# k^T v on both partition halves: by products through the identity, or by copies

## The chip, the cores and the metric

The kernel runs on one core of a Trainium2 chip. A core has a matrix engine (TensorE, PE in the profile; PEld is its loading of weights), VectorE (DVE), ScalarE (ACT), GpSimd (POOL) and SyncE (SP), which here only issues transfers. Each engine works through its own instructions in order and waits on semaphores that the others raise. TensorE writes only to PSUM, a small memory of banks; ScalarE and VectorE read it from there. The metric is the time of one execution on the device in microseconds (us); lower is better.

## The reference

Attention without a softmax over 8 batches of 8 heads, 576 positions and 64 channels, then a mixture of eight experts on its output:

```python
kv = np.einsum('bhsd,bhse->bhde', k, v)
out = np.einsum('bhsd,bhde->bhse', q, kv)
rms = np.sqrt(np.mean(out * out, axis=-1, keepdims=True) + 1e-06)
x = (out / rms * g_norm)           # then (B,H,S,D) -> (B*S, H*D)
...
skip_score = x @ w_skip; logits = x @ w_gate
...
out[do_compute] = x + gate_w * (relu(x @ w1[e]) @ w2[e])
```

All of the change is in the first line and in what the second reads: the 64 x 64 matrix kv of each head. Everything is in fp32.

## The kernel before

The kernel has an attention stage (up to about 118 us) and an expert stage. Its order of instructions is written out by hand: inside `tc.manual_schedule()` each engine gets its instructions in the order of the program text, and the framework adds the semaphores.

**kv of a batch.** `state(b, some)` forms k^T v of the eight heads of batch b on TensorE, in 72 products of 64 x 64 (line 380) into the PSUM tile `sum_ps`. There is one such tile. A product in fp32 shows as two records in the profile. When the last is done, two ScalarE copies (line 387) put the sums into `own(b, w)`: heads with w = 0 into partitions 0 to 63 of the tile `kvd`, heads with w = 1 into partitions 64 to 127. `kvd` holds for each head a block diagonal matrix of two blocks, one per partition half, so that one product of 128 rows can serve two positions at once; so the same numbers have to stand on the other half as well (`kvds[b % KVD][o, :, w, 1 - w, :]`). Beside kv each block has 2 x 9 more columns ("ends"), kv times the weights of the skip score and of the eight gates, so that the routing comes out of the same product as the attention.

Three functions finish a batch:
- `state_t(b)`: four products with the identity (line 394) turn kv into `kvT_ps`, a ScalarE copy takes it to `kvT` (line 397).
- `state_m(b)`: two products of kvT with the gate weights (line 403) give the ends in `lg_ps`, two small ScalarE copies (line 406) put them into `own`.
- `state_s(b)`: two products with the identity (line 412) move the finished block, 292 columns with its ends, to the other partition half in PSUM (`sw_ps`), and two ScalarE copies (line 416) put it into `kvd`.

**Units.** The second line of the reference runs in 36 units n, four per batch and two extra ones after every four batches (units 16, 17, 34, 35) for the ninth block of positions. A unit has these parts: `turn(n)`, four transposes of q (line 461) and a ScalarE copy to qT (line 464); `values(n)`, four products of 128 rows (line 499; line 509 for the extra units) into a bank of `o_ps`, of which there are two, and a ScalarE square of them (line 515); in a batch's first two units two more transposes (line 480) and a copy (line 483) prepare the ninth block. Then `squares(n)` (VectorE reduction, line 523), `root(n)` (ScalarE, line 530), `norm(n)` (VectorE reciprocal and scaling into `xl`, lines 537 and 546, which frees the bank), and `finish(n)` on GpSimd (lines 598 to 616). The stores follow.

**The loop's order.** Step n of the main loop issues: turn(n+1), root(n-1), the jobs put at "early", values(n), the jobs at "mid", norm(n-1) and squares(n), the jobs at "pe", finish(n-1), the jobs at "dve" and "end". The kv work of the batches is spread over the steps as such jobs: the table `portions` says at which step the products of a batch begin and how many go in each step. state_t stands in the step behind the last of them: step 3, 7, 10, 14, 20, 24, 28 for b = 1 to 7. A batch's values begin at n = 4, 8, 12, 18, 22, 26, 30. The next batch's products begin at step 4, 7, 11, 16, 20, 24, so for b = 2, 5 and 6 they start in the step of that batch's own state_t. The gating of tokens (line 663 and on) runs beside this as further jobs, mostly on VectorE with small products on TensorE.

**Loads.** SyncE issues all loads of k, v and q in quarters of a batch (line 118), with three buffers for k and v and two for q, the stores, and later the experts' weights.

Of the kernel before, what the change touches and what calls it, by code (L numbers as in the profile page):

```python
# [17 lines left out]
def kernel(  # L18
# [43 lines left out]
    nc = tc.nc  # L62
    B, H, S, D = q.shape
# [10 lines left out]
    G = E + 1  # L74
# [4 lines left out]
    PK = 2 * KD  # L79

    KVD = 5
# [28 lines left out]
    g_ps = ps_g.tile([P, 512], FP32)  # L110
# [17 lines left out]
    def load_kv(b, js=range(4)):  # L128
        if b < B:
            if js.start == 0:  # L130
                for name, to in (("k", kts), ("v", vts)):
                    to[b] = kv_pool.tile([P, 4, C, D], FP32, tag=name, name=name)
            for j in js:
                for src, t in ((k, kts[b]), (v, vts[b])):
                    load_part(t, src, b, j)

    def load_q(b):
        if b < B:
            qts[b] = load(q_pool, "q", q, b)
# [61 lines left out]
    ident = keep.tile([P, P], FP32)  # L201
# [3 lines left out]
    kvds = []  # L205
# [27 lines left out]
    for a in range(2):  # L233
        r = slice(a * 64, (a + 1) * 64)
# [60 lines left out]
    for lo, m, _ in runs:  # L295
# [26 lines left out]
        out=srow[:, :].rearrange("p (r c) -> p r c", c=CK),  # L322
# [33 lines left out]
    def own(b, w):  # L356

        return kvds[b % KVD][w * 64:(w + 1) * 64, :, w, w, :]

    sum_all = ps_kv.tile([P, 2, 512], FP32, name="sum_ps")  # L360
    sum_ps = sum_all[:, :, 0:2 * D].rearrange("p a (u d) -> p a u d", u=2)
    sw_ps = g_ps[:, 0:2 * PK]
    kvT_ps = g_ps[:, 0:2 * P].rearrange("p (u x) -> p u x", u=2)
    lg_ps = g_ps[:, 2 * PK:2 * PK + 8 * G].rearrange("p (u a w g) -> p u a w g", u=2, a=2, w=2)

    def ends_of(x):

        ap = [list(d) for d in x.ap]
        assert ap[-1] == [1, PK]
        return bass.AP(x.tensor, x.offset, ap[:-1] + [[PK - G, 2], [1, G]])  # L370

    def state(b, some):

        kt, vt = kts[b], vts[b]
        for i in some:
            u, c = divmod(i, C)
            for w in range(2):
                for a in range(2):
                    r = slice(a * 64, (a + 1) * 64)
                    nc.tensor.matmul(  # L380
                        out=sum_ps[w * 64:(w + 1) * 64, a, u, :],
                        lhsT=kt[r, 2 * u + w, c, :], rhs=vt[r, 2 * u + w, c, :],
                        start=(c == 0), stop=(c == C - 1), skip_group_check=True)
        if some.stop < 2 * C:
            return
        for w in range(2):
            nc.scalar.copy(out=own(b, w)[:, :, G:G + 2 * D].rearrange("p u (a d) -> p a u d", a=2),
                           in_=sum_ps[w * 64:(w + 1) * 64, :, :, :])

    def state_t(b):  # L390
        for u in range(2):
            for w in range(2):
                r = slice(w * 64, (w + 1) * 64)
                nc.tensor.matmul(out=kvT_ps[:, u, r], lhsT=kvds[b % KVD][:, u, w, w, G:G + 2 * D],  # L394
                                 rhs=ident[:, r], start=True, stop=True)
        kvT = att_pool.tile([P, 2, P], FP32, tag="kvT", name="kvT", bufs=1)
        nc.scalar.copy(out=kvT[:, :, :], in_=kvT_ps)
        kvTs[b] = kvT

    def state_m(b):  # L400
        kvT = kvTs.pop(b)
        for u in range(2):
            nc.tensor.matmul(out=lg_ps[:, u, :, :, :], lhsT=kvT[:, u, :], rhs=gw_b[:, u, :, :, :],
                             start=True, stop=True)
        for w in range(2):
            nc.scalar.copy(out=ends_of(own(b, w)), in_=lg_ps[w * 64:(w + 1) * 64, :, :, w, :])

    def state_s(b):

        for w in range(2):  # L410
            r, o = slice(w * 64, (w + 1) * 64), slice((1 - w) * 64, (2 - w) * 64)
            nc.tensor.matmul(out=sw_ps[o, :], lhsT=ident[r, r], rhs=own(b, w), start=True, stop=True,  # L412
                             skip_group_check=True)
        for w in range(2):
            o = slice((1 - w) * 64, (2 - w) * 64)
            nc.scalar.copy(out=kvds[b % KVD][o, :, w, 1 - w, :],
                           in_=sw_ps[o, :].rearrange("p (u k) -> p u k", u=2))


    units = []  # L420
# [22 lines left out]
    def at(step, part, job):  # L443
        todo.setdefault((step, part), []).append(job)
# [7 lines left out]
    def turn(n):  # L452
        _, b, i, u = units[n]
        if i is None:
            qTs[n] = q8s[b][:, u, :, :, :]
            return
        ps = ps_q.tile([P, 2, 2, 2, 64], FP32, tag="q", name="q_ps")
        for w in range(2):
            for hf in range(2):
                c = 4 * i + 2 * hf  # L460
                nc.tensor.transpose(out=ps[:, w, :, hf, :], in_=qts[b][:, 2 * u + w, c:c + 2, :],  # L461
                                    identity=ident[:, :])
        qT = att_pool.tile([P, 2, 2, P], FP32, tag="qT", name="qT")
        nc.scalar.copy(out=qT[:, :, :, :].rearrange("p w a t -> p (w a t)"),
                       in_=ps[:, :, :, :, :].rearrange("p w a h t -> p (w a h t)"))
        qTs[n] = qT
# [478 lines left out]
    for b in range(KNOWN // S // 4 * 4, KNOWN // S):  # L945
        nc.gpsimd.dma_start(
            out=out[b * S:(b + 1) * S, :].rearrange("(p c) d -> p c d", c=C)[:, C - 1, :],
            in_=zero)

    starts = {}  # L950
    for n, (_, b, i, _) in enumerate(units):
        if i is not None:
            starts.setdefault(b, n)
    state(0, range(C))
    dense(4)
    state(0, range(C, 2 * C))
    dense(5)
    state_t(0)
    turn(0)
    state_m(0)  # L960
    turn(1)
    state_s(0)

    portions = {1: (1, (10, 8)), 2: (4, (6, 6, 6)), 3: (7, (5, 6, 7)), 4: (11, (5, 6, 7)),
                5: (16, (8, 4, 3, 3)), 6: (20, (4, 4, 5, 5)), 7: (24, (4, 4, 5, 5))}
    over = 0
    for b, n in starts.items():
        if b:
            step, counts = portions[b]
            i = 0  # L970
            for count in counts:
                at(step, "early" if step in (starts[1], starts[2], starts[4] - 2) else "pe",
                   lambda b=b, some=range(i, i + count): state(b, some))
                i += count
                step += 1
            assert i == 2 * C and step < n and step - len(counts) > over - 1
            last = b == B - 1
            at(step, "mid" if last else "early", lambda b=b: state_t(b))
            at(*((step + 1, "early") if last else (step, "pe")), lambda b=b: state_m(b))
            at(step + 1, "early" if step + 1 == n else "pe", lambda b=b: state_s(b))  # L980
            over = step
        at(over, "end", lambda b=b: load_kv(b + 3, range(4 if b else 2)))

        at(n + 2, "end", lambda b=b: load_q(b + 2))
        if b == 0:
            at(n + 2, "end", lambda: load_kv(3, range(2, 4)))
# [73 lines left out]
    with tc.tile_pool(name="wpool_b", bufs=1, reuse_waits="tile") as wpool_b, \  # L1060
# [522 lines left out]
        with tc.If(n_rounds > 1):  # L1583
            with tc.For_i(1, n_rounds, 1):
# [8 lines left out]
                    out=left[:, :].rearrange("p (r c) -> p r c", c=CK),  # L1593
# [39 lines left out]
```

## Time and profile before

| | |
|---|---|
| three runs | 370.62, 371.28 (median), 371.82 us |
| the profiled execution | 372.36 us, of which the span from the first to the last instruction is 370.6 us |
| granted TensorE clock | 0.999 of full speed |
| TensorE busy | 358.2 us, 97% of the span |
| VectorE, ScalarE, GpSimd busy | 242.3, 151.5, 118.6 us (65%, 41%, 32%) |
| from 20 to 60 us: TensorE busy per 10 us | 9.63, 10.00, 10.00, 9.93 |
| the same, ScalarE | 6.21, 6.76, 7.29, 7.14 |
| the same, VectorE | 5.28, 5.64, 4.99, 6.52 |
| from 90 to 120 us: VectorE per 10 us | 8.76, 8.00, 8.91 |
| the same, ScalarE | 7.79, 6.92, 7.75 |
| line 412 (state_s), TensorE | 32 records, 0.405 to 0.457 us each |
| line 416, ScalarE copies of 292 columns | 16, 0.397 to 0.400 us each |
| line 387, ScalarE copies of 256 columns | 16, 0.371 to 0.378 us each |

A busy share is an average over the whole span and over stages with different limits; it does not say what sets the end. The chain that ended last does: from the last instruction it goes back, at each step, to what released it or to the instruction before it on its engine. In rows of the chain the first number is the start in us from the span's beginning and the second how long the piece lasts; "issue" is time in which the engine waited for nothing that the profile shows. In rows of a timeline the brackets give how long the engine was idle before and which instruction ended that. Records of matmuls overlap, since they are pipelined and their ends are modelled; the distance from one start to the next is the better measure of what a group costs.

### The profile page before, as it was taken

The page shows a single profiled execution, that of the slowest core. Times are in us where ns is not written, and L with a number is a line of the kernel's source. Part 1 is how long each engine was busy: PE and PEld are TensorE (multiplying, and loading weights), DVE is VectorE, ACT ScalarE, POOL GpSimd, SP SyncE. Part 2 cuts the span into 40 slices and gives each one's busy share as a digit, 9 for nine tenths or more (in the row PEclk, how much of TensorE's full clock was granted, in tenths as well). Part 3 has the DMA queues.
Part 4 walks back from the last instruction along what each step waited for, and adds up shares of the span by engine and source line. Part 5 has one row for each costly group of instructions (what it writes and reads, how often), then busy time and mean ns, then how long its engine had stood idle before and what let it go on. Part 6 is the DMA issues. An engine that isn't in the chain of part 4 may idle for free.

```text
span 370.6 us, 9688 instructions
## 1 busy us (share of the span) xinstructions
PE 358.2 (97%) x3835; PEld 312.8 (84%) x3835; DVE 242.3 (65%) x621; ACT 151.5 (41%) x426; POOL 118.6 (32%) x189
## 2 busy tenths in 40 slices
PE   8999999899999998999999999999999999999994
PEld 4688998798889667589879988988988988999983
DVE  3255557767878761786847675776776876878831
ACT  2467676666767151434303511431530430441420
POOL 8036466655777062223021203303203202002003
PEclk9999999999999999999999999999999999999999
DMA  8999999999598449963617355563662672701001
GB/s 267 387 389 389 396 391 381 385 369 351 182 307 315 113 139 375 384 216 120 227 44 261 79 214 170 189 229 99 222 251 70 232 251 71 240 2 43 17 1 54
DMA packets 32809, 81.72 MB, mean 221 GB/s; under 512 B 3242, under 2 KB 3250, under 8 KB 32756
## 3 DMA queue, kind: packets, MB, share of 16 engines
q1 hardware_dynamic: 28944, 69.48, 53.0%
q0 software_dynamic: 3792, 11.53, 9.4%
q8 instruction: 32, 0.52, 0.6%
q14 instruction: 21, 0.17, 0.1%
q10 hardware_dynamic: 20, 0.02, 0.0%
HBM read 66.80 MB, written 14.48 MB: 219 GB/s over the span
## 4 chain that ended last, share of the span: by engine, by line
PE 83%; issue 6%; DMA 5%; ACT 2%; POOL 2%; DVE 1%; SPq 1%; POOLq 0%; ACTq 0%; DVEq 0%
PE bank L1257 45%; PE bank L1189 9%; PE o_ps L499 7%; PE sum_ps L380 4%; PE bank L1177 4%; PE q_ps L461 3%; PE bank L1158 2%; DMA v<-in_v_dram 2%; PE g_ps L394 2%; DMA q<-in_q_dram 2%; DMA k<-in_k_dram 1%; PE o_ps L480 1%; PE g_ps L857 1%; PE g_ps L412 1%; PE q_ps L857 1%
## 5 line engine op out<-in xcount | busy, mean ns | idle before, releaser
L1267 ACT COPY p<-bank 128x128 f32<-128x128 f32 (+6 forms) x70 | 20.9, 298 | 96.2 <-PE bank L1257 94.7
L1257 PE MATMUL bank<-xt,w 128*128 128x128 f32 (+5 forms) x336 | 55.5, 288 | 0.5 <-DVE bank L1261 0.5
L1388 POOL DMA_INDIRECT out_dram<-xg,rows x14 | 14.0, 1000 | 116.6 <-DVE xg L1385 114.4
L616 POOL TENSOR_TENSOR xb<-xl,g_b 128x512 f32<-128x512 f32 x34 | 41.3, 1216 | 29.6 <-DVE rs L537 27.7
L1257 PEld LDWEIGHTS bank<-xt,w 128*128 128x128 f32 x336 | 47.0, 190 | 2.4 <-DVE bank L1261 1.9
L1261 DVE TENSOR_TENSOR bank<-bank,p 128x128 f32<-128x128 f32 (+6 forms) x70 | 23.6, 337 | 30.0 <-PE bank L1257 28.9
L499 PE MATMUL o_ps<-kvd,qT 128*128 128x146 f32 x240 | 36.0, 290 | 1.1 <-issue 0.8
L1257 PE MATMUL bank<-xs,s 128*128 128x128 f32 (+5 forms) x224 | 36.7, 288 | 0.0
L523 DVE TENSOR_REDUCE rs<-sq 128x8 f32<-128x512 f32 x36 | 24.5, 681 | 15.7 <-ACT sq L515 15.6
L499 PEld LDWEIGHTS o_ps<-kvd,qT 128*128 128x128 f32 x240 | 31.6, 189 | 1.7 <-issue 1.1
L1257 PEld LDWEIGHTS bank<-xs,s 128*128 128x128 f32 x224 | 31.1, 190 | 1.0 <-issue 0.5
L1189 PE MATMUL bank<-w,ht 128*32 128x128 f32 (+2 forms) x424 | 29.9, 313 | 0.0
L546 DVE TENSOR_TENSOR xl<-o_ps,rs 128x584 f32<-128x584 f32 x32 | 24.5, 767 | 4.3 <-DVE rs L537 0.5
L1189 PEld LDWEIGHTS bank<-w,ht 128*32 128x32 f32 (+2 forms) x424 | 18.2, 119 | 10.6 <-issue 7.2
L1257 PE MATMUL bank<-t,ht 128*128 128x256 f32 x112 | 27.0, 384 | 0.0
L1257 PE MATMUL bank<-w,ht 128*128 128x256 f32 x112 | 26.5, 380 | 0.0
L515 ACT ACTIVATE sq<-o_ps 128x512 f32<-128x512 f32 x34 | 20.3, 597 | 15.1 <-PE o_ps L499 14.9
L380 PE MATMUL sum_ps<-v,k 64*64 64x64 f32 x1152 | 25.3, 222 | 0.8 <-DMA v<-in_v_dram 0.8
L1257 PE MATMUL bank<-t,hs 128*128 128x256 f32 x112 | 25.3, 379 | 0.0
L380 PEld LDWEIGHTS sum_ps<-v,k 64*64 64x64 f32 x1152 | 21.6, 134 | 4.3 <-issue 2.2
L1149 POOL DMA_INDIRECT xg<-out_dram,src x14 | 14.0, 998 | 34.9 <-DMA out_dram<-xg,rows 12.7
L1257 PEld LDWEIGHTS bank<-t,ht 128*128 128x128 f32 x112 | 20.8, 190 | 3.9 <-issue 1.2
(217 smaller groups left out, 676.5 us busy)
## 6 DMA issues: line engine op xcount, KB each, us to landing
w<-in_moe_w_dram SPq DMA_DIRECT2D x16, 2048.0 KB, 14.1
k<-in_k_dram SPq DMA_DIRECT2D x32, 288.0 KB, 6.0
v<-in_v_dram SPq DMA_DIRECT2D x32, 288.0 KB, 7.2
q<-in_q_dram SPq DMA_DIRECT2D x32, 288.0 KB, 5.7
out_dram<-xb SPq DMA_DIRECT2D x29, 256.0 KB, 6.0
out_dram<-xb POOLq DMA_DIRECT2D x7, 256.0 KB
xg<-out_dram,src POOLq DMA_INDIRECT x16, 3.4
out_dram<-xg,rows POOLq DMA_INDIRECT x16, 2.5
```

The source lines that it names most:

```text
L380: nc.tensor.matmul(out=sum_ps[w * 64:(w + 1) * 64, a, u, :], lhsT=kt[r, 2 * u + w, c, :], rhs=vt[r, 2 * u + w, c, :], start=(c == 0), stop ...
L499: mm = nc.tensor.matmul(out=ps[:, w, 0:2 * PK].rearrange("p (r k) -> p r k", r=2)[:, :, cols], lhsT=qT[:, w, a, :], rhs=kvds[b % KVD][:, u ...
L515: nc.scalar.activation(out=sq[:, :, :, :], in_=heads(ps, G, G + 2 * D), func=ACT.Square)
L523: nc.vector.tensor_reduce(out=rs[:, :, :], in_=sq[:, :, :, :].rearrange("p x y (a d) -> p x (y a) d", a=2), axis=AX.X, op=ALU.add)
L546: nc.vector.tensor_tensor(out=xl[:, :, :, :].rearrange("p x y (a k) -> p x (y a) k", a=2), in0=ps[:, :, 0:2 * PK].rearrange("p x (h k) -> ...
L616: late.append((lambda eng: eng.tensor_tensor(out=xb[:, :, 4 * u * D:(4 * u + 4) * D].rearrange("p r (w x) -> p r w x", w=2), in0=xl[:, :, ...
L1149: nc.gpsimd.indirect_dma_start(out=x_of(xg, off, m), out_offset=None, in_=cut_rows(m)[:, :], in_offset=bass.IndirectOffsetOnAxis(ap=idx[:, ...
L1177: nc.tensor.matmul(out=hps[:, cols], lhsT=w_sb[r][0][:, dc, f * P:(f + 1) * P], rhs=xt[:, dc, cols], start=(dc == 0), stop=(dc == DC - 1))
L1189: nc.tensor.matmul(out=yps[q * m:(q + 1) * m, 0:n], lhsT=ht(f)[:, off:off + m], rhs=w_sb[r][1][:, f, q * n:(q + 1) * n], start=(f == 0), s ...
L1257: nc.tensor.matmul(out=out, lhsT=lhsT(i), rhs=rhs(i), start=start and i == 0, stop=i == k - 1, skip_group_check=True)
L1261: nc.vector.tensor_tensor(out=to, in0=x, in1=y, op=ALU.add)
L1267: nc.scalar.copy(out=t, in_=x)
```

## The change

`state_s` goes. The other partition half is now filled straight from `sum_ps` by ScalarE copies that read one half and write the other (`put_sums(b, other)`, two copies of 256 columns, issued behind the copy of kvT in state_t), and the ends are put into both halves by four small copies in place of two. `sum_ps` is thus read a second time, later than before. And where there is a step between the kv work and the batch's first unit (b = 3 to 6; for b = 7 it was so already), state_t moves from "early" to "mid", behind values(n), and state_m from "pe" to the "early" of the next step; for b = 1 and 2 state_t stays and state_m moves from "pe" to "mid".

```diff
+    def other(b, w):
+
+        return kvds[b % KVD][(1 - w) * 64:(2 - w) * 64, :, w, 1 - w, :]
+
+    def put_sums(b, half):
+        for w in range(2):
+            nc.scalar.copy(out=half(b, w)[:, :, G:G + 2 * D].rearrange("p u (a d) -> p a u d", a=2),
+                           in_=sum_ps[w * 64:(w + 1) * 64, :, :, :])
+
...
-        for w in range(2):
-            nc.scalar.copy(out=own(b, w)[:, :, G:G + 2 * D].rearrange("p u (a d) -> p a u d", a=2),
-                           in_=sum_ps[w * 64:(w + 1) * 64, :, :, :])
+        put_sums(b, own)
...
         nc.scalar.copy(out=kvT[:, :, :], in_=kvT_ps)
+        put_sums(b, other)
         kvTs[b] = kvT
...
-        for w in range(2):
-            nc.scalar.copy(out=ends_of(own(b, w)), in_=lg_ps[w * 64:(w + 1) * 64, :, :, w, :])
-
-    def state_s(b):
-
-        for w in range(2):
-            r, o = slice(w * 64, (w + 1) * 64), slice((1 - w) * 64, (2 - w) * 64)
-            nc.tensor.matmul(out=sw_ps[o, :], lhsT=ident[r, r], rhs=own(b, w), start=True, stop=True,
-                             skip_group_check=True)
-        for w in range(2):
-            o = slice((1 - w) * 64, (2 - w) * 64)
-            nc.scalar.copy(out=kvds[b % KVD][o, :, w, 1 - w, :],
-                           in_=sw_ps[o, :].rearrange("p (u k) -> p u k", u=2))
+        for half in (own, other):
+            for w in range(2):
+                nc.scalar.copy(out=ends_of(half(b, w)), in_=lg_ps[w * 64:(w + 1) * 64, :, :, w, :])
...
-    state_s(0)
...
-            last = b == B - 1
+            last = step + 1 < n
             at(step, "mid" if last else "early", lambda b=b: state_t(b))
-            at(*((step + 1, "early") if last else (step, "pe")), lambda b=b: state_m(b))
-            at(step + 1, "early" if step + 1 == n else "pe", lambda b=b: state_s(b))
+            at(*((step + 1, "early") if last else (step, "mid")), lambda b=b: state_m(b))
```

More of the change, by code (lines that the diff above doesn't have):

```diff
@@ L358, in own @@
         return kvds[b % KVD][w * 64:(w + 1) * 64, :, w, w, :]
+    def other(b, w):
[4 more added lines that the diff above has]
+                           in_=sum_ps[w * 64:(w + 1) * 64, :, :, :])
     sum_all = ps_kv.tile([P, 2, 512], FP32, name="sum_ps")
     sum_ps = sum_all[:, :, 0:2 * D].rearrange("p a (u d) -> p a u d", u=2)
-    sw_ps = g_ps[:, 0:2 * PK]
     kvT_ps = g_ps[:, 0:2 * P].rearrange("p (u x) -> p u x", u=2)
```

## The prediction

> **What bounds the kernel now.** I read the page first (engine shares, the chain that ended last), then the chain in order of time for the attention stage, then the timelines of TensorE, ScalarE, VectorE and of SyncE's queue there.
>
> ```profile
> PE 83%; issue 6%; DMA 5%; ACT 2%; POOL 2%; DVE 1%; SPq 1%; POOLq 0%; ACTq 0%; DVEq 0%
> 13.69 7.26 DMA v<-in_v_dram
> 20.95 0.14 issue
> 21.08 0.33 PE sum_ps L380 x4
> ```
>
> The chain is TensorE's for 83% of the span. The first line is the page's, the others are the chain in order of time (start, duration, what). Its DMA share is the start alone: up to 20.95 us the chain is a load, and the products of batch 1 wait for it. So nothing that is saved for batch 0 (before 20.95) moves the end. From there on TensorE is the path, but two things can take its place, and both show in the trace.
>
> The first is the loads. In the table of ten-microsecond windows the DMA share is 1.03 to 1.05 from 10 to 80 us. The first row below is from SyncE's timeline (start, duration), the second closes the view of the tile q and tells how long its loads take:
>
> ```profile
> 42.56 1.20 SPq L118 DMA_DIRECT2D q<-in_q_dram  x2
> DMA to landing us min/median/max: 4.9/5.7/5.8
> ```
>
> The transfer issued at 42.56 is the second quarter of q of batch 3. With 5.8 us it lands at about 48.4. The transposes of unit 12 read it, and TensorE starts them at 48.74 (the half that needs this quarter some 0.2 later). TensorE can be about half a microsecond earlier there, and no more. Later loads have 3 us and more.
>
> The second is the seam after batch 3, where for 7 us the chain runs over ScalarE, VectorE and GpSimd, and then shows a stall of TensorE that no semaphore explains:
>
> ```profile
> 60.05 0.61 ACT sq L515
> ...
> 62.80 0.60 DVE rs L523
> ...
> 66.14 0.78 DVE xl L546
> ...
> 66.96 0.41 PE o_ps L480 x2
> 67.36 0.38 PE o_ps L499 x3
> 67.74 0.85 issue
> ```
>
> The square of unit 14, the reduction of unit 15 and the scaling of unit 16 hand the path on, until unit 18 gets a bank at 66.96.
>
> **The products that go.** The chain in batch 2's place:
>
> ```profile
> 39.82 0.59 PE q_ps L461 x4
> 40.41 0.21 PE g_ps L412
> 40.62 0.17 PE sum_ps L380 x5
> 40.79 0.26 PE g_ps L412 x2
> 41.05 0.70 PE sum_ps L380 x38
> ```
>
> L412 is `state_s`. The two products are 0.43 us each, side by side and partly beside the products of the next batch. I measure from start to start: transposes of unit 9 at 39.75, next work at 41.67, so 1.92. Without `state_s` it is 0.59 + 0.86 (48 records of L380, as at 32.32 to 33.17) = 1.45: 0.47 saved. In batch 1 it is 2.17 - 1.45 = 0.72, since L412 also waits there for the small copies. Then the load of q caps it: the 1.19 so far cannot all be kept. The half of unit 12's transposes that reads the second quarter starts at 48.45 in place of 48.96; 0.24 for that half, 0.45 for `state_m`, 1.10 for the values of unit 11 and 0.74 for 40 records of L380 follow, so unit 13 is turned at 50.98 in place of 51.53. **Gain so far 0.55.**
>
> **The copies.** Two of 292 columns per batch go (0.40 each); two of 256 (0.37, L387) and two of 36 (0.19) come. ScalarE has 0.3 us more per batch and is 60 to 78% busy, so what matters is where they stand. They read one partition half and write the other, which no copy out of PSUM does before. The nearest row:
>
> ```profile
> L1117 ACT COPY moved<-srow x14: 190/192/198, 127.0 to 131.8; 64x1 f32<-64x1 f32 x4, 32x2 f32<-32x2 f32 x4, 32x3 f32<-32x3 f32 x4, 64x2 f32<-64x2 f32 x2
> ```
>
> By the code some of these cross partitions and some stay, and all take 190 to 198 ns. So the bounds are 0.37 (nothing extra) and, with no row above it, twice that; I take 0.37. In batches 1 and 2 `put_sums` fits a hole of 0.74 us on ScalarE before the square, and the next batch's first product comes later: no cost.
>
> **Turned behind the values, batches 3 to 6.** Before, `state_t` stood behind the transposes and waited for the copies of the sums:
>
> ```profile
> 72.24 0.66 PE L461 MATMUL q_ps<-ident,q 128*128 128x128 f32 x4
> 73.07 1.28 PE L394 MATMUL g_ps<-ident,kvd 128*128 128x64 f32 x8 [0.18 <-ACT kvd L387]
> 74.19 1.22 PE L499 MATMUL o_ps<-kvd,qT 128*128 128x146 f32 x8
> 75.25 0.53 PE L403 MATMUL g_ps<-gw_b,kvT 128*128 128x36 f32 x4
> 75.70 0.69 PE L380 MATMUL sum_ps<-v,k 64*64 64x64 f32 x32
> ```
>
> It takes 1.12 (73.07 to 74.19), because its third record waits for the second copy, and 0.3 goes before it. Batch 7 already has the other order, and there it takes 0.83 (98.22 to 99.05). This is the gain of the move, some 0.6 a batch. The price is new: **`sum_ps` has one buffer, and the next batch's products must wait until `put_sums(b, other)` has read it.** Batch by batch:
> - b=4 (step 14): the square of unit 14 starts at 58.8 in place of 60.05, `state_t` ends at 59.5, kvT and the two copies at 60.66. The root of unit 14, queued behind them, runs at 60.7 in place of 61.40. No transposes stand between `state_t` and `state_m` here, so TensorE waits 0.46 for kvT, but the path is VectorE's: the reduction of unit 15 starts at 62.45 in place of 62.80. The seam moves by about 0.3. **Gain 0.3.**
> - b=5 (step 20): `state_t` ends at 74.74, kvT 75.2, copies 76.0. Batch 6's products stand next on TensorE (75.70 before) and idle until then: 1.2 us. All of step 20 and 21 is 72.24 to 79.02 = 6.78 before; after it is 0.49 + 1.01 + 1.0, the wait, 0.6 for the products, 0.55 + 0.45 + 1.10 + 0.52 = about 6.9. **Loss 0.1.** ScalarE's root of unit 20 slips by 0.5; values of unit 22 need its bank only 0.6 later.
> - b=6: the same, 7.50 before, 7.62 after. **Loss 0.1.**
> - b=7: order unchanged, `state_s` alone cost 0.64 to 0.72 (101.33 to 101.97). But ScalarE then has 1.15 us more between kvT and the square of unit 29 (before at 101.43, idle 0.61 ahead of it; after, 101.9). The reduction of unit 29, the table `bv` behind it on VectorE and the 22 small products (103.70) follow that square. **Gain 0.25.**
>
> SyncE and GpSimd are passed by nothing: no DMA changes its place in the order, and the loads are paced by the engines' throughput. The expert stage follows the attention stage's end; its chain is TensorE's and no load ends a wait in it.
>
> **The stall of 0.85.** It falls in the middle of four products whose operands are ready. A window view of 66 to 69 us shows
>
> ```profile
> q8 instruction: 1, 0.02, 2.3%
> ```
>
> one 16 KB packet of the instruction queue (32 in the whole run[...]). [...] the sum is 0.55 + 0.3 - 0.1 - 0.1 + 0.25 = **0.9 us**. By the row it is a fetch that came late in the densest stretch (32 L509 products in 0.67 us, twice). Then it moves: five `state_s` (4 products and 4 weight loads each, 40 records) are gone ahead of it, the block ends 40 records later, after the rest of the values and 30 records of L380 (about 1.0 us) in place of 40 records of L509 (0.43), so the fetch has 0.55 more and the stall falls to 0.3. Ends: 0 and 0.85. I follow the row, since among 32 fetches this is the only stall of its size without a releaser while products are ready: **0.55**. A fetch may also fall badly elsewhere; that is in the range.
>
> **Sum:** 0.9 + 0.55 = 1.4 us. Against the profiled execution: span 370.6, its time 372.36, so 1.76 around the span; 369.2 + 1.76 = 371.0. The runs shown have the median 371.28, 1.1 below the profiled one; on that base I forecast **369.9 us**, just over the 0.3% (1.1 us) that a measurement of this kernel can tell from no change.
>
> **Rivals.**
> - *No measurable change, 22%.* The q load takes 0.7 us of the first savings anyway, [...] the stall stays: 370.4 to 371. For it: every other term is small and of both signs. Against: 16 products less on a path that is TensorE's.
> - *ScalarE holds the output banks, slower, 20%.* `o_ps` has two buffers; values of unit n+2 wait for unit n's scaled values, these for its root, and the root now stands behind kvT and two copies in batches 3 to 7. I find 0.1 us of slack left in batch 5. If the root comes a further 0.7 late (two or three extra semaphore waits, or crossing copies at twice the price), TensorE waits 0.6 in each of five batches: 3.0 - 0.9, so 373.4; it decides from about 0.3 us of further delay on. For it: VectorE is without a hole from 95.7 to 103 us. Against: before, ScalarE idles 0.2 to 0.75 ahead of most squares.
> - *The forecast, 56%* (0.9 to 2.5 us gained). The rest, 2%, is a gain of more than that.
>
> The range takes the stall gone wholly and a load 0.3 earlier at one end, half of the slow rival at the other: 368.7 to 372.4. Faster 0.57, same 0.22, slower 0.21.
>
> **What would show it.** L412 gone; L387's successor with 32 copies of 0.37; TensorE idle before unit 12's transposes, with a q load as releaser; TensorE idle about 1.2 us ahead of L380 in batches 6 and 7 with ScalarE's copies as releaser; state_t at about 0.83; the gap at 67.7 smaller or elsewhere. Wrong if TensorE waits for VectorE before values in several batches, or if the crossing copies are not at 0.37.

## The result and the profile after

| | before | after |
|---|---|---|
| median (lowest to highest), 8 runs each | 371.39 (370.45 to 371.82) us | 374.47 (372.45 to 376.52) us |
| ratio, with its 95% interval | | 1.0088 [1.0061, 1.0115] |
| the profiled execution, its span | 372.36, 370.6 us | 372.52, 370.7 us |
| TensorE busy; ScalarE busy | 358.2; 151.5 us | 353.4; 153.7 us |

The kernel became 0.9% slower; the forecast was 369.9 us, with a range of 368.7 to 372.4. TensorE has 4.8 us less work and the time is 3 us longer. Ratios are of fast executions: one that took over 1.5% more than the fastest of its kernel is left out of them (five of the 22 of bv_first, one each of after_again and early_56). The profiled execution of after is the second fastest of its eight, so a difference of the two spans says nothing here: stages have to be compared, and more than one profile. The page's chain by engine, of after:

```profile
PE 81%; issue 6%; DMA 5%; ACT 3%; DVE 2%; POOL 1%; SPq 1%; POOLq 0%; DVEq 0%; ACTq 0%
```

TensorE lost 2 points, ScalarE and VectorE have one each. TensorE's waits from 20 to 119 us (for what; us in total, times, longest) have two large ones in after that before does not have at all:

```profile
PE sum_ps L388 <- ACT kvd L366: 2.5, 2, 1.2
PE g_ps L919 <- DVE bv L899: 1.2, 1, 1.2
```

The chain in order of time (start, duration, what) shows where ScalarE came in. Batch 5's place in after:

```profile
74.92 0.85 PE g_ps L400 x8
...
75.80 0.37 ACT kvT L403
...
76.18 0.37 ACT kvd L366
...
76.56 0.38 ACT kvd L366
...
76.98 0.79 PE sum_ps L388 x31
```

TensorE ends the turn of the sums (L400) at 75.77 and stands until 76.98, while ScalarE does three copies one after another; only the last one frees `sum_ps` for batch 6's products (L388). Behind these products stand, in TensorE's own queue, the transposes of unit 22, so they are late as well. Batch 6 has the same picture (88.43 to 89.66), and two waits more. TensorE's timeline there, before:

```profile
84.12 0.66 PE L461 MATMUL q_ps<-ident,q 128*128 128x128 f32 x4
84.98 1.28 PE L394 MATMUL g_ps<-ident,kvd 128*128 128x64 f32 x8 [0.21 <-ACT kvd L387]
86.10 1.22 PE L499 MATMUL o_ps<-kvd,qT 128*128 128x146 f32 x8
```

and after (the last row is of its weight loads):

```profile
85.47 0.66 PE L458 MATMUL q_ps<-ident,q 128*128 128x128 f32 x4
86.32 1.27 PE L496 MATMUL o_ps<-kvd,qT 128*128 128x146 f32 x8 [0.19 <-DVE xl L543]
...
91.60 0.52 PEld L410 LDWEIGHTS g_ps<-gw_b,kvT 128*128 128x128 f32 x4 [0.22 <-DVE top L709]
```

The values of unit 24 (L499, now L496) need the bank that VectorE's scaling of unit 22 frees. In both kernels it is free 0.81 us after the start of the transposes ahead of them (at 84.93 and 86.28). Before, the turn of the sums (L394) fills that time; in after it stands behind the values, and TensorE waits. So it is the move that lays this wait open, and not a late root on ScalarE: in both kernels the root of unit 21 starts 1.2 us after its step's transposes. In the last row `state_m` (L410), now a step later, stands behind small products of the gating that write the same PSUM tile, and waits until VectorE has read their result (`top`, L709). Batch 7, the chain of after again:

```profile
104.17 0.60 ACT sq L512
...
104.79 0.69 DVE rs L520
105.48 1.01 DVE bv L899
...
106.53 0.71 PE g_ps L919 x22
```

TensorE waits 1.23 us here for `bv`, a small VectorE product.

How long each place takes, from the start of one unit's transposes to that of another, is the same in all four profiles taken of before within 0.02 us (11.65, 10.05 and, from unit 30 to the first product of unit 35, the last one, 13.97 us). So a difference of 0.05 us can be read there. These places are used as a ruler below:

| kernel, less before, in us | batch 5 (unit 20 to 24) | batch 6 (24 to 27) | batch 7 (30 to 35) | ratio to before |
|---|---|---|---|---|
| after, four profiles | +0.32 to +0.33 | +0.90 to +0.92 | +0.52, +0.52, +3.05, +2.21 | 1.0088; again 1.0048 [1.0024, 1.0071] |
| copies_only | -0.45 | -0.04 | +2.14 | 1.0007 [0.9979, 1.0035] |
| move_only | -0.59 | -0.01 | -0.01 | 1.0009 [0.9988, 1.0029] |
| copies_early | -0.93 | -0.42 | +0.18 | 0.9955 [0.9936, 0.9975] |
| copies_early_2 | -0.94 | -0.41 | +0.17 | 0.9970 [0.9947, 0.9993] |
| early_56 | -0.93 | -0.42 | +0.52 | 0.9976 [0.9954, 0.9998] |
| early_7 | +0.32 | +0.91 | +0.18 | 1.0047 [1.0020, 1.0073] |
| early_unmoved | -0.29 | -0.04 | +0.18 | 1.0003 [0.9973, 1.0034] |
| after_pad | +0.39 | +0.91 | +2.21 | 1.0076 [1.0044, 1.0108] |

### The profile page after: what moved, and what is told of

Read it like the earlier page. It is cut to its first block, busy times and chain, and to the rows that moved or that the text cites. A ratio compares the mean times of both kernels' runs of the same rounds, so it can differ in the third digit from the quotient of the medians.

```text
span 370.7 us, 9630 instructions
## 1 busy us (share of the span) xinstructions
PE 353.4 (95%) x3803; PEld 310.2 (84%) x3803; DVE 243.6 (66%) x621; ACT 153.7 (41%) x442; POOL 119.3 (32%) x189
## 4 chain that ended last, share of the span: by engine, by line
PE 81%; issue 6%; DMA 5%; ACT 3%; DVE 2%; POOL 1%; SPq 1%; POOLq 0%; DVEq 0%; ACTq 0%
PE bank L1252 45%; PE bank L1184 9%; PE o_ps L496 6%; PE sum_ps L388 4%; PE bank L1172 4%; PE q_ps L458 3%; PE bank L1153 2%; DMA v<-in_v_dram 2%; DMA q<-in_q_dram 2%; PE g_ps L400 2%; DMA k<-in_k_dram 1%; PE g_ps L854 1%; ACT kvd L366 1%; ACT qT L461 1%; PE o_ps L477 1%
## 5 line engine op out<-in xcount | busy, mean ns | idle before, releaser
L496 PE MATMUL o_ps<-kvd,qT 128*128 128x146 f32 x240 | 35.8, 289 | 1.4 <-issue 1.2
L496 PEld LDWEIGHTS o_ps<-kvd,qT 128*128 128x128 f32 x240 | 31.6, 189 | 1.7 <-issue 1.3
L388 PE MATMUL sum_ps<-v,k 64*64 64x64 f32 x1152 | 23.8, 222 | 4.5 <-ACT kvd L366 2.5
L388 PEld LDWEIGHTS sum_ps<-v,k 64*64 64x64 f32 x1152 | 19.9, 134 | 8.7 <-issue 3.2
L461 ACT COPY qT<-q_ps 128x512 f32<-128x512 f32 x32 | 18.7, 585 | 13.0 <-PE q_ps L458 12.6
```

The lines of the kernel that those rows point to most:

```text
L388: nc.tensor.matmul(out=sum_ps[w * 64:(w + 1) * 64, a, u, :], lhsT=kt[r, 2 * u + w, c, :], rhs=vt[r, 2 * u + w, c, :], start=(c == 0), stop ...
L496: mm = nc.tensor.matmul(out=ps[:, w, 0:2 * PK].rearrange("p (r k) -> p r k", r=2)[:, :, cols], lhsT=qT[:, w, a, :], rhs=kvds[b % KVD][:, u ...
```

## The experiments

The kernels were run in groups, each group on one chip beside runs of before, to which its ratios belong. Before, run once more as if it were another kernel (before_again), has the ratio 0.9985 [0.9958, 1.0012].

### Either edit alone, and the copies put elsewhere

copies_only has the copies in place of the products, with the turn in the steps of before:

```diff
-            last = step + 1 < n
+            last = b == B - 1
...
-            at(*((step + 1, "early") if last else (step, "mid")), lambda b=b: state_m(b))
+            at(*((step + 1, "early") if last else (step, "pe")), lambda b=b: state_m(b))
```

> The copies in place of the products, but state_t and state_m at the steps of before (state_t at early, state_m at pe; batch 7 as ever). Theory ORDER (the copies behind kvT hold sum_ps and ScalarE's queue once state_t stands behind the values; 1.7 us of the loss are in batches 5, 6 and 7): the next batch's products now come after the values again, so the waits of 1.2 us ahead of them go, and the time is about that of before, 370.5 to 371.5. Theory FETCH (TensorE stands still at the border of a 256-record block whose packet comes late among the loads; 3.5 us of such stalls in the profile after against 0.85 before): the products saved let TensorE run ahead of its blocks just the same, so stalls of 0.5 to 1.2 us at records 194 modulo 256 stay, the time is 372 to 374 and spreads by more than 1 us from run to run.

move_only is before with the turn behind the values and the products kept (`last = step + 1 < n` alone):

> The products of state_s stay, only the steps of state_t and state_m are those of the change. ORDER: sum_ps is not read late, nothing waits for it, and state_t behind the values takes 0.83 in place of 1.12 and hides the wait for the copies: 0.5 us gained in each of four batches less the wait for kvT in batch 4, so 369.5 to 370.5. FETCH: the record count is that of before, borders fall where they fell, but TensorE is up to 1 us ahead of before at them: one or two stalls more than before, 371.5 to 373.

copies_early is after with the crossing copies right behind the first two:

```diff
         put_sums(b, own)
+        put_sums(b, other)
...
         nc.scalar.copy(out=kvT[:, :, :], in_=kvT_ps)
-        put_sums(b, other)
```

> The change, with the two copies into the other half issued right behind those into the own half, so sum_ps is free before state_t begins. ORDER: the waits of 1.2 us ahead of L380's products in batches 6 and 7 and the late square of unit 29 go: 1.5 to 2 us less than the change, 372 to 373. FETCH: three stalls of about 1.2 us stay, since they lie before these places; 373.5 to 375, spread as wide as after's.

after_again is after, beside them:

> The changed kernel once more, for a second profile and its times. FETCH: again several stalls of TensorE without a releaser, each at a record whose number is 194 modulo 256, but not all at the same blocks; the time 372 to 376. ORDER: the same waits ahead of the products of batches 6 and 7 as in the first profile, 1.2 us each, and few stalls at block borders; the time within 0.5 us of 374.5.

Measured: 371.41, 371.35, 369.72 and 372.88 us, beside 370.83 us for before. Each edit alone is equal to before; both together are slower; both together with the two copies moved up behind the first two are the fastest kernel of the study. The ruler says why. In batch 5 each edit alone gains (0.45, 0.59 us), and together they lose 0.33. In copies_only the turn stands ahead of a unit's values, and these products cover the copies behind kvT. The move takes that cover away. In batch 6 each edit alone gains next to nothing (0.04, 0.01): the profiles of move_only and copies_early show the waits for the bank and for `top` as in after, so they come with the move, and in copies_only the gating's products wait 0.48 us for the small copies of the ends. Copied early, the sums are read while TensorE is at the values ahead of the turn; the chain of copies_early, where after waited:

```profile
75.22 0.84 PE g_ps L401 x8
76.06 0.62 PE sum_ps L388 x32
76.68 0.59 PE q_ps L458 x4
```

Between the turn and the next batch's products there is no gap, and the products take 0.62 us for 32 records where after needed 0.79 for 31 behind its wait.

### Which batch it is

early_56 puts the copies early in batches 5 and 6 alone, early_7 in batch 7 alone:

```diff
         put_sums(b, own)
+        if b in (5, 6):
+            put_sums(b, other)
...
-        put_sums(b, other)
+        if b not in (5, 6):
+            put_sums(b, other)
```

> The crossing copies stand right behind the first two copies in batches 5 and 6 alone, elsewhere as in after. Theory 'the order' (ScalarE's two copies behind kvT hold back the products of the next batch, and the root behind them the banks): of the 3.2 us that moving the copies in all batches regained, 2.6 come from these two, so a ratio to before of about 0.998 and some 370.2 us on a chip where before is 370.8; unit 22 is turned about 1.2 us earlier than in after. Rival 'the fetch' (the stalls at 42, 62 and 68 us make the loss): these stalls lie ahead of both edits or beside them, so the ratio stays at 1.005 to 1.009.

> The crossing copies stand right behind the first two in batch 7 alone. Theory 'the order': the two copies of 0.38 leave the stretch from kvT to the square of unit 29, whose followers end in the wait of the 22 small products; about 0.5 us are regained if that wait is on the path, 0.3 by the profiles so far: a ratio of 1.004. Rival 'the fetch': nothing, 1.005 to 1.009.

early_56: 370.32 us against 371.21 of before, ratio 0.9976, where 0.998 was expected. By the ruler both batches are as in copies_early. So the loss of these two batches, 2.6 us in the profile (0.33 + 0.93 and 0.91 + 0.42), is shown in the times as well: 0.7% between the ratio of early_56 and those of after_again (1.0048) and of early_7, which ran on the same chip (1.0047). early_7: 372.7 us; the ruler gives the 0.34 us expected, and the time can't tell that from nothing.

### What the move is worth then

early_unmoved has all copies together and the turn in the steps of before, beside copies_early a second time:

> All copies of the sums stand together, the crossing ones behind the first two, and the turn of the sums stands in the steps where before has it (ahead of the values). Theory 'the move pays once the copies are out of its way': before waits some 0.3 us in each of batches 3 to 6 between the transposes and state_t, and 0.3 us more inside state_t; this kernel does so still, so it is 1.2 to 2 us slower than copies_early beside it: a ratio to before of about 0.999 to 1.001. Rival 'the gain comes from the products that go and the move is worth nothing' (move_only was equal to before): as fast as copies_early, 0.995 to 0.997.

> copies_early a second time, beside early_unmoved. Both theories: a ratio to before of 0.994 to 0.998 again. If it is 1.000 or above, the version is no better than before after all.

371.3 and 369.78 us, with 370.77 for before. The intervals overlap, so the 1.2 us between the ratios (as expected) is likely rather than shown; the ruler has 0.64 us of it in batch 5 and 0.37 in batch 6.

### The stalls without a releaser

Three in the chain of after (start, duration, what), then three in that of a second profile of before:

```profile
43.80 1.17 issue
...
63.28 1.19 issue
...
70.00 0.63 issue
```

```profile
23.78 0.80 issue
...
44.39 1.36 issue
...
70.69 0.71 issue
```

Counted through TensorE's list (products, weight loads and its semaphore instructions), every one stands at a record whose number is 194 more than a multiple of 256 (in after 1474, 2242 and 2498), as the one of the prediction does (2498). In after a 16 KB packet of the instruction queue ends at 43.50, 62.95 and 69.17, and TensorE goes on at 44.97, 64.47 and 70.63, 1.5 us later; in the first profile of before 67.29 and 68.59.

The next two kernels leave out the loads of k and v from batch 3 on and of q from batch 2 on, and compute with the tiles that are there; the expert stage then has other work, so only the attention stage is read:

> The kernel before without the loads of k and v from batch 3 on and of q from batch 2 on: later batches use the tiles of batches 0 to 2 again, so their part of the result is another, and the routing may need further rounds; only the attention stage, up to the first L1177 product, is to be read. FETCH: with the DMA engines no longer full after 30 us the stall of 0.85 at 67.7 goes. Other theories: it stays.

> The changed kernel with the same loads left out, to be read beside the one before it. FETCH: no stall at a block border is left from 35 us on, and the attention stage ends within 0.3 us after, or before, that of before_noload, since 3.5 us of stalls against 0.85 made the difference of 2.8. ORDER: the waits for sum_ps and for ScalarE are there without loads too, and the attention stage still ends 1.5 to 2 us later than in before_noload.

They took 708.46 and 709.53 us. Before had no stall at a border at all, after one of 0.70 at 23.2 us, while loads were still running. The packet that ends at 43.50 in after starts at 42.46, and the same packet starts at 37.6 in both kernels without the loads; it takes about 1.0 us in all of them. So with the loads the packet starts 4.9 us later and TensorE stalls, and without them it does neither; that TensorE stands for this packet is read from these times and not shown by itself. Without the loads the steps of the sum can be read: at unit 20 after is 0.95 us ahead, batch 5 takes 0.29 back and batch 6 0.82, batch 7 and what follows 3.0 (its clock dropped, see below); at unit 35 after is 3.2 us behind. That is more than the 1.5 to 2 of 'ORDER', by the drop of the clock: without it batch 7 would be at +0.52, as in two profiles of after, and the end at some 0.7 (an estimate from these figures).

after_pad writes the first nine products, whose results are not used, as 36 of a quarter of the columns:

```diff
-    dense(9)
+    for _ in range(36):
+        nc.tensor.matmul(out=warm_ps[:, 0:P], lhsT=ones[:, :], rhs=ones[:, :], start=True, stop=True)
```

> The nine products of 512 columns at the start, which compute nothing that is used, are written as 36 of 128 columns: the same columns, 27 products and 27 weight loads more, so 54 more of TensorE's instructions ahead of everything. Theory of the stalls (a block of 256 instructions that comes late): TensorE's stalls without a releaser are again at records 194, 450, 706 and so on of its list, which are now instructions 54 records earlier in the program, so that they stand at other times (some 1 to 2 us earlier each); the time may go either way by up to 2 us. Rival (the stall belongs to an instruction or to a wait that the records don't show): the stalls stay with the same instructions, now at records 760, 1528, 2296 and 2552.

It has one stall without a releaser, of 2.2 us, and it stands at record 2498; there is none at 760, 1528, 2296 or 2552. So the border decides and not the instruction, as far as one stall can show it: record 2498 is a transpose here, a product of the sums in after. At 706 and 1474 there was none this time. The time, 373.82 us, is that of after.

Then the question whether the change makes the stalls longer:

> The kernel before, profiled a second time. The first profile of before has its attention stage 2.8 us shorter than that of after, and its expert stage 2.75 us longer, with three stalls of TensorE at 140.6 to 143.6 us and one at 239.5 us. Theory 'the order': those stalls are a chance of that one execution, so this profile has an expert stage of about 255 us and a span of 368 to 369 us. Rival 'the expert stage gives back what the attention stage gains': the stage is about 257.6 us again and the span 370.6 us.

> The kernel before, a third profile. Theory 'chance' (how long TensorE stands at a border of 256 instructions is drawn anew in every execution, in both kernels alike): the stalls at the borders up to 119 us sum to 2 to 4 us, as in its second profile (3.1 us) and not as in its first (0.85 us). Theory 'the change' (with fewer instructions ahead, after meets the borders at worse places): 0.5 to 1.5 us, against 3.5 us in after.

> The kernel after, a third profile. Theory 'chance': stalls of 2 to 4 us. Theory 'the change': 3 to 4 us again.

> As before_3: 'chance' 2 to 4 us of stalls at the borders, 'the change' 0.5 to 1.5 us.

> As after_3: 'chance' 2 to 4 us, 'the change' 3 to 4 us. If the means of four profiles of each kernel lie within 0.5 us, the stalls have no part in the difference of the medians.

Stalls without a releaser at the borders sum, in the attention stage, to 0.85, 2.9, 2.3 and 2.6 us in four profiles of before, and to 3.5, 3.6, 1.6 and 2.4 in four of after. The first profile of before, the only one that the prediction had, is the odd one. The means, 2.2 and 2.8 us, lie 0.6 apart, a little more than the 0.5 that was set as the bound, and without that one profile 0.2. A part of up to half a microsecond stays open; the growth from 0.85 to 3.5 us is not the change's doing. before_again also shows that the expert stage of the first profile of before was long: 257.6 us there, 254.9 here and in after. Its own span was 370.7 us and not 368 to 369, since the attention stage had 2.8 us more, mostly stalls.

### Batch 7: a small product that waits, and what follows it

The tile view of `bv` on VectorE (count, ns min/median/max), first before, then after:

```profile
L902 DVE TENSOR_TENSOR bv<-ohc,row_k x1: 243/243/243, 102.9 to 102.9; 128x88 bf16<-128x88 bf16 x1
```

```profile
L899 DVE TENSOR_TENSOR bv<-ohc,row_k x1: 1085/1085/1085, 105.4 to 105.4; 128x88 bf16<-128x88 bf16 x1
```

The same product takes four times as long. GpSimd's timeline of after has, at that moment,

```profile
105.20 1.17 POOL L613 TENSOR_TENSOR xb<-xl,g_b 128x512 f32<-128x512 f32 x1
```

It ends at 106.37, `bv` (from 105.40) at 106.48. In before `bv` starts at 102.92 and that product 0.03 us later, and `bv` takes 0.24:

```profile
102.95 1.26 POOL L616 TENSOR_TENSOR xb<-xl,g_b 128x512 f32<-128x512 f32 x1
```

In every profile where the crossing copies of batch 7 stand behind kvT (all four of after, copies_only, early_56, after_pad, after_noload) `bv` takes 1.08 to 1.10 us; in every other one up to here 0.24. The order of the two decides which, where both starts were read: `bv` takes 0.24 us where it starts 0.01 to 0.03 us ahead of GpSimd's product (before, copies_early, early_7), and 1.08 to 1.09 where it starts 0.20 or 0.21 us behind it (after, after_3, after_4), ending 0.1 us after it. What holds `bv` there was not shown. Measured against the transposes of unit 30, the square of unit 29 is 0.49 us late, `bv` starts 0.23 us late for it and ends 1.07 us late.

Then TensorE's clock. The windows of after and of after_3 (us, busy time and count of PE, PEld, DVE, ACT, POOL; then the granted clock, DMA share, GB/s):

```profile
104.00:106.00 2.00, 1.30 (x11) 1.12 (x10) 1.88 (x3) 1.70 (x5) 2.00 (x3) 1.00 1.03 342
106.00:108.00 2.00, 1.21 (x27) 1.12 (x27) 1.15 (x5) 0.66 (x2) 0.38 (x1) 1.00 0.97 385
```

```profile
104.00:106.00 2.00, 0.80 (x23) 0.71 (x22) 1.18 (x3) 1.07 (x3) 0.79 (x1) 1.00 1.00 383
106.00:108.00 2.00, 2.00 (x10) 2.00 (x11) 1.85 (x6) 0.62 (x2) 1.07 (x1) 0.51 1.03 414
108.00:110.00 2.00, 2.00 (x13) 2.00 (x12) 0.50 (x2) 0.42 (x2) 1.46 (x3) 0.64 0.61 203
```

Behind the same idle stretch (a wait of 1.24 us, the 22 small products, another of 0.25) the clock was halved for some 3 us in after_3, and not in after. after_4, after_pad, copies_only and after_noload show the drop too, after_again and early_56 don't, and none of the four profiles of before does. That is the step from +0.52 to +2.2 and +3.05 in the ruler's last column. Over all timed executions, a mean clock below 0.9955 is had by 41 of 73 of the four kernels in which `bv` takes 1.08 us (15 of 30 of after), by 13 of 92 of the five in which it takes 0.24, and by 14 of 178 of before. Among the 22 of after_again the 9 below it took 373.8 us on average, the other 13 took 371.8; in early_56 it is 371.3 (12) and 369.4 (10).

To test it, `bv` was put right behind `ohc`, three instructions earlier on VectorE; no other queue changes its order:

```diff
                                 op=ALU.is_equal)
-        yield
         bv = gat_pool.tile([P, NE, 2, 2], BF16, tag="bv1", name="bv1")
...
                                 op=ALU.mult)
+        yield
         ps = g_ps[:, GB:GB + 4]
```

> After with one change: VectorE's small product bv (L899 in after) stands right behind ohc, three instructions earlier, out of the way of GpSimd's xb. Nothing else in any queue changes. In six profiles of kernels that keep batch 7's copies behind kvT, and in four of after among them, bv takes 1.08 us and ends with xb; elsewhere 0.24 us. Theory 'GpSimd holds bv, and the idle TensorE loses its clock': bv takes 0.24 us, TensorE's wait ahead of the 22 small products falls from 1.23 us to under 0.4 us, a granted clock below 0.9955 is had by less than a quarter of the executions (15 of 30 in after), and the ratio to before falls from 1.005 to 1.009 to about 1.002. Rival 'the order of the copies alone makes the loss, the clock is a chance': half of the executions below 0.9955 again and a ratio of 1.005 to 1.009.

> Both edits: the crossing copies of batches 5 and 6 stand right behind the first two, and bv right behind ohc. Theory 'two causes': as fast as copies_early, a ratio of 0.993 to 0.996, with few executions below a clock of 0.9955 (12 of 22 in early_56). Rival 'order alone': 0.9976 as early_56.

`bv` takes 0.25 us in both, TensorE waits for nothing ahead of the 22 products, and from unit 30 to 33 they are 0.88 and 0.87 us faster than before, where after is 0.52 slower: so it is the place behind GpSimd's product that makes `bv` long (in bv_first it starts at 103.6, and that product at 104.08). What this does to the time is not shown. bv_first's ratio is 1.0022 [1.0000, 1.0044], as expected, but 8 of its 22 executions are below the clock of 0.9955, not under a quarter, and its median over all is 375.22 us against 373.42 of before. early_56_bv has 0.9968 [0.9948, 0.9987] (expected 0.993 to 0.996; early_56 had 0.9976). Their profiles show a new wait. The chain of early_56_bv:

```profile
105.01 6.64 DMA xg<-out_dram,src
...
111.78 0.45 PE q_ps L846 x2
```

The second gather of token rows, whose indices these 22 products bring, takes 6.6 us (6.8 in bv_first, whose profiled execution took 377.34 us) where it takes 3.0 to 4.2 in before, after, copies_early and early_56. TensorE waits 2.3 us for it, and its clock drops right behind (0.51 from 112 to 114 us in early_56_bv and from 116 to 118 in bv_first). Both kernels issue this gather earlier; whether it meets other transfers for that reason, or because of this chip, was not tried. So that the clock drops far more often where TensorE waits for `bv` is shown; that this wait makes it drop is likely and not shown.

## The prediction, point by point

It had 0.9 us of gain from the order of work and 0.55 from the stall. Three terms failed: batch 6 (a loss of 0.1; measured 0.91), batch 7 (a gain of 0.25; measured a loss of 0.52, and of 2.2 or more where the clock dropped) and the stall (a gain of 0.55; measured none).

- **"Gain so far 0.55" and batch 4's 0.3.** Right step by step: batch 1 gives 0.74 us (from unit 5 to 6) and batch 2 0.48 (9 to 10), in after and in the pair without loads alike, where 0.72 and 0.47 were worked out; batch 4 gives 0.34 without loads. The cap by q of batch 3 is there in after_4 and after_pad; in the three other profiles of after a stall at 44 to 45 us had taken the lead away first. TensorE's weight loads in after_4:

```profile
48.38 0.20 PEld L458 LDWEIGHTS q_ps<-ident,q 128*128 128x128 f32 x2 [0.48 <-DMA q<-in_q_dram]
```

- **The copies.** Taken at 0.37 us with no surcharge for crossing, measured 0.37 to 0.38. `state_t` behind the values was taken at 0.83, measured 0.84 to 0.85. "Some 0.6 a batch" for the move shows as 0.59 in batch 5 of move_only; in batch 6 it is nothing, so a gain that was read off one batch was given to all.
- **Batch 5, "loss 0.1": +0.33.** The wait for `sum_ps` was named, and is 1.21 us as worked out. The term "0.6 for the products" behind it was 0.73 from start to start (0.79 as a row of the chain); the rest is spread over the small terms.
- **Batch 6, "the same ... loss 0.1": +0.91.** This term failed. It was copied from batch 5 and not worked out with its own neighbours. Of the 0.58 us by which batch 6 is worse than batch 5, the wait for the bank is 0.46: the values of unit 24 start 0.85 us after the transposes ahead of them where batch 5's start after 0.49, and take 0.10 longer. The wait of `state_m` for `top` is 0.23 more, and 0.10 comes off, which before itself spends there. Both waits come from the move, which took the turn from the one and put `state_m` behind the gating for the other; the forecast had both at nothing. With the 0.2 that it missed in batch 5 too, this is the whole of the miss.
- **Batch 7, "gain 0.25": +0.52 or more.** This term failed in its logic. The square of unit 29 was placed right (101.43 + 0.47, and 2.25 for the shift so far: 104.15; measured 104.17). But the saving of `state_s` on TensorE was set against its delay, although the 22 products wait for VectorE, whose path runs through that square: the saving could not count there (early_7, without the late square and with `bv` at 0.24, is still at +0.18). That `bv` could come to stand behind GpSimd's product, and that the clock could drop behind the hole, was not seen.
- **The stall, 0.55 gained.** Wrong, and not for what it made of the row: the runs show the stalls at borders of 256 instructions, 1.3 to 1.5 us behind the end of a packet, and only beside the loads (the 256 is read from the distances of the stalls; 32 packets over all of its records would be about 240 each). Wrong was to take one execution's 0.85 us for the kernel's: in the seven other profiles of the two kernels the sum is 1.6 to 3.6 us.
- **The sum with what was measured:** by the four profiles of each kernel, stalls included, after is on average 0.7 us ahead at unit 20, and -0.7 + 0.33 + 0.91 + 1.6 (mean of four for batch 7 and its tail) = +2.1 us at unit 35. The two comparisons of after with before give +1.8 and +3.3 us; why the larger is 1.2 us above the sum stays open.

The rival "ScalarE holds the output banks" had the right side and nearly the time (373.4). Its engine was right and its mechanism was not: in batches 5 and 6 the root stands as far behind the transposes as before (1.2 us), and the bank's wait in batch 6 comes from the move. What ScalarE's copies hold is `sum_ps`, named in the forecast itself as a price, and the square in batch 7. That its number came near is luck.

## What to carry to other kernels

A copy that frees a buffer belongs as early in its engine's queue as its data allow: two copies of 0.37 us, four instructions later on ScalarE in batches 5 to 7, turned a gain of 0.3 to 0.45% into a loss of 0.5 to 0.9%. Two edits that each cost nothing can cost together, when one is the cover of the other, and a piece of work that is moved lays open the waits it covered; so price each with the other in place, and each loop iteration with its own neighbours. And before a stall is booked, profile the kernel twice.

## What the runs showed of the hardware

- TensorE stalled at borders of 256 of its instructions, for up to 2.2 us (after_pad); the DMA share in those of the first profiles of before and after is 1.00 to 1.06. The stalls differ from execution to execution (0.85 to 3.6 us in the attention stage of eight profiles), and behind 24 us there is none where the loads are left out.
- VectorE's product of 88 columns took 0.24 us where it started up to 0.03 us ahead of a GpSimd product of 1.26 us, and 1.08 to 1.09 where it started 0.20 or 0.21 us behind one of 1.17 to 1.19.
- Behind a wait of 1.24 us, 22 small products and a wait of 0.25, TensorE's clock was halved for some 3 us in five of eight profiles with that wait (in after_3 a mean of 0.51 and 0.64 in two stretches of 2 us), and stayed at 1.00 in the other three.
